# Layer norm, gated MLP and long convolution with gradients: tile 0's norm reordered, tiles 4 and 5 turned by transfers

## The chip, the cores and the metric

One core of a Trainium2 chip. The time is device microseconds of one execution, the median of three timed runs. A separate, profiled execution gives the trace; its times count from the start of its span.

The names are those of the profile. PE is the matrix engine, PEld its weight loads, DVE the vector engine, ACT the scalar engine, POOL the general-purpose engine, and SP the engine that here does nothing but issue transfers. SP's transfers run on queue q1, ACT's on q10, POOL's on q0; all share 16 DMA engines. A transfer is issued by an instruction in the issuing engine's own order, and lands later.

## The reference

The forward pass normalizes the rows of an input, feeds them to a long convolution (branch A) and to a gated MLP (branch B), and adds the results to the input. The kernel returns this output and the gradients of nine inputs for a given `grad_out`.

```
x  = A_q                                  # 2048 x 1024
xn = (x - mean(x)) / sqrt(var(x) + 1e-5)  # per row
A  = xn * (causal_conv(kv, ssm_k) + kv * ssm_D),   kv = shift_conv(k, shift_k) * v
gate, up = xn @ W_gate, xn @ W_up         # 1024 x 3584 each
B  = (relu(gate) * up) @ W_down           # 3584 x 1024
out = x + A + B
grads = vjp of the above for grad_out
```

## The kernel before

The 2048 rows are 16 row tiles of 128. All is bf16 with fp32 accumulation in PSUM. PE runs almost without a pause in this order: `hidden` (gate, up and the gradient of the hidden layer), `grad_down`, `grad_in`, `out_phase`, `grad_x`. Matmuls of branch A are put between those of the first three, at a pace counted in estimated nanoseconds.

The part that is changed is the first of the 14 passes of `hidden` (n = 0, rows 0 to 1023, first 512 of the 3584 hidden columns). For each of its eight row tiles s it needs:

- `gate(s)` and `up(s)`: eight 128x512 matmuls each, with the transposed normalized tile `xnT` as weights and `wg` or `wu` as moving operand (`gemm8`, the matmul at line 1092). ACT takes relu of the gate result, DVE masks the up result and multiplies.
- `grad_row(s)`: eight matmuls with the transposed gradient tile `goT` as weights and `wdT` as moving operand. ACT copies the result to `gh`, DVE multiplies it into the stored pair `ru`.

In this pass nothing is there beforehand: the input tiles are loaded (`ln_load`), normalized (`layer_norm`), transposed (`flip_xn`) and used. `layer_norm` is a generator, and each `next(ln)` moves it one step on; `chunk` takes several steps. Tiles 0 to 3 are normalized singly, the others in pairs. For tile 0, DVE makes mean and variance (`stats`); `root` adds epsilon on DVE and takes the root, and a scaled copy, on ACT; `inverse` makes the reciprocal on DVE. `sums` is an ACT pass with an accumulated sum, and tile 1's mean and variance come from three such passes.

`flip_xn(st)` has two ways. Tiles 0 to 5: eight PE transposes into PSUM (line 1135), then copies to `xnT` by DVE, or by ACT for tile 4 (line 1140). Tiles 6 and 7: a transposing transfer from the normalized tile to `xnT`, issued by SP (line 1128). `goT` and `wdT` are always made by transposing transfers from DRAM.

The order on PE before is: 12 warming matmuls, tile 0's transposes, gate 0, half of up 0, then (by `first_mid`, called after the fourth matmul of up 0) tile 1's transposes, gate 1, up 1, tile 2's transposes, the other half of up 0, gate 2, half of up 2, tile 3's transposes, the other half, gate 3, up 3. Gradient rows 0 and 1 follow, with the transposes of tiles 4 and 5 in the middle of row 1 (`flip_ahead(0)`), then gates and ups 4 and 5, gradient rows 2, 3, 4 and 5 (with `flip_ahead(2)`, which issues the transfers of tiles 6 and 7), gates and ups 6 and 7, and gradient rows 6 and 7.

The order of the work on each engine comes from a scheduler with priorities (`Pri`); instructions given to `keep_in_program_order` stay as written, and `issue_after` puts a bound on when a transfer may be issued. Each engine runs its queue in order. SP's queue at the start is: half of input tile 0, `wg` x4, `wu` x2, input tile 2, `wu` x2, tile 3, `wdT` x2, tiles 4 and 5 in one transfer, `wdT` x2, `goT` 0 and 1, tiles 6 and 7 in one transfer, `goT` 2 and 3, the shift weights `sk_b`, the next pass's `wg` x4, `goT` 4 to 7, `xnT` 6 and 7, the next `wu` x4.

Branch A starts its own loads at a pace set in `ABranch.steps`: filter, gradient (`load_g`), v (`load_v`, tile `vt`), k (`load_taps`), normalized rows (`load_xn`, tile `xt`, read back from DRAM).

Of the kernel before, what the change touches and what calls it, by code (L numbers as in the profile page):

```python
# [14 lines left out]
ALU = mybir.AluOpType  # L15
ACT = mybir.ActivationFunctionType
AX = mybir.AxisListType
P = 128
# [3 lines left out]
class Pri:  # L22
# [9 lines left out]
    def pin(self, ins, always=False):  # L32

        if self.strict or always:
            self.tc.keep_in_program_order(ins)
# [13 lines left out]
class ABranch:  # L49
# [545 lines left out]
    def steps(self):  # L595

        sk_t = self.shift_rows()
        self.pin = True  # L600
        yield 10000
        self.load(self.sk_d, sk_t[:])
        yield 25000
        self.sts = [dict(gi=gi, cg=slice(gi * P, (gi + 1) * P)) for gi in range(self.NG)]
        st = self.sts[0]
        self.load_filter(st)
        self.issue()
        yield 3400
        self.load_g(st)
        yield 3400  # L610
        self.load_v(st)
        yield 3400
        self.load_taps(st)
        yield 6800
        self.load_xn(st)
        self.pin = False
        self.pri.strict = True
        self.open_arena()
        for st in self.sts:
            for p, d in self.slots(st, st["gi"]):  # L620
                *more, last = self.parts(p)
                for fs in more:
                    self.tensor(fs)
                    yield self.DENSE[0]
                self.tensor(last)
                self.run(d)
                self.stores()
                for e in self.queue:
                    e[2] -= 1
                if self.queue and self.queue[0][2] <= 0 and not self.hold():  # L630
                    self.issue()
                yield self.DENSE[p is None] if self.dense else self.SLOT
        while self.out:
            self.stores()
# [238 lines left out]
class LnMlp:  # L873
# [7 lines left out]
    def open_left(self):  # L881
        tc = self.tc
        self.per = tc.alloc_tile_pool(name="b_per", bufs=1, side="left")
        self.actp = tc.alloc_tile_pool(name="b_act", bufs=1, side="left")
        self.w2 = tc.alloc_tile_pool(name="b_w2", bufs=1, side="left")
        self.e2 = tc.alloc_tile_pool(name="b_e2", bufs=6, side="left")
        self.e1 = tc.alloc_tile_pool(name="b_e1", bufs=6, side="left")
        self.ps = tc.alloc_tile_pool(name="b_ps", bufs=8, space=bass.MemoryType.PSUM)
        self.ln_x, self.xn, self.todo, self.kept, self.hold, self.busy = [], [], [[]], [], False, False
        self.rstd = self.per.tile([P, self.ST], F32, name="rstd")  # L890
        self.ident = self.per.tile([P, P], BF16, name="ident")
        make_identity(self.nc, self.ident[:])
# [55 lines left out]
    def layer_norm(self, xn_d, jpool, jtag, spool):  # L948
# [9 lines left out]
        def sums(out, x, func, **kw):  # L958
            jk = jpool.tile([P, D], BF16, name="ln_j", tag=jtag)
            return act(jk[:, 0:x.shape[-1]], x, func, accum_out=out, **kw)  # L960
# [12 lines left out]
            else:  # L973
                quarter(V.tensor_scalar(out=sm[:, 5, 0:n], in0=smb[:, 2, 0:n], scalar1=0.25, scalar2=None, op0=ALU.mult))

        def inverse(sm, smb, n, st0, pin):
            pin(V.reciprocal(out=sm[:, 6, 0:n], in_=sm[:, 4, 0:n]))
            if n == 1:
                V.scalar_tensor_tensor(out=smb[:, 3, 0:n], in0=sm[:, 6, 0:n], scalar=sm[:, 5, 0:n], in1=sm[:, 4, 0:n],
                                       op0=ALU.mult, op1=ALU.add)  # L980
            else:
                V.tensor_tensor(out=sm[:, 5, 0:n], in0=sm[:, 5, 0:n], in1=sm[:, 6, 0:n], op=ALU.mult)
                V.tensor_tensor(out=smb[:, 3, 0:n], in0=sm[:, 4, 0:n], in1=sm[:, 5, 0:n], op=ALU.add)
            self.ln_dve = V.reciprocal(out=self.rstd[:, st0:st0 + n], in_=smb[:, 3, 0:n])
# [24 lines left out]

        for _ in stats(x0, b0):  # L1010
            pass
        sums(s1[:, 0, 0:1], x1[:, 0:h], ACT.Copy, scale=-1.0 / D)
        root(s0, b0, 1, hold, None)
        hold(V.tensor_scalar(out=b0[:, 3, 1:2], in0=b0[:, 0, 0:1], scalar1=-1.0, scalar2=None, op0=ALU.mult))
        hold(V.tensor_scalar(out=x0[:, 0:h], in0=x0[:, 0:h], scalar1=b0[:, 0, 0:1], scalar2=None, op0=ALU.subtract))
        hold(act(x0[:, h:D], x0[:, h:D], ACT.Identity, bias=b0[:, 3, 1:2]))
        hold(sums(s1[:, 1, 0:1], x1[:, h:D], ACT.Copy, scale=-1.0 / D))
        hold(act(b1[:, 0, 0:1], s1[:, 1, 0:1], ACT.Identity, bias=s1[:, 0, 0:1]))
        hold(sums(s1[:, 2, 0:1], x1, ACT.Square, bias=b1[:, 0, 0:1]))
        inverse(s0, b0, 1, 0, hold)  # L1020
        self.pri.now()
        for k in range(2):
            hold(scale(x0[:, k * h:k * h + h], 0))
# [11 lines left out]
        st0 = 2  # L1035
# [88 lines left out]

    def flip_xn(self, st):
        xT = self.act_tile("xnT", st)
        if st > 5:
            self.turned = self.nc.sync.dma_start_transpose(out=xT[:].rearrange("p (a b) -> p a b", b=P),
                                                           in_=self.xn[st])
            return xT  # L1130
        h = self.DT // 2 if st < 3 else self.DT
        for k0 in range(0, self.DT, h):
            pst = self.ps.tile([P, self.DT, P], BF16, name="pst_x", tag="bps")
            for kt in range(k0, k0 + h):
                self.pri.pin(self.nc.tensor.transpose(pst[:, kt, :], self.xn[st][:, kt * P:(kt + 1) * P],  # L1135
                                                      self.ident[:]), always=True)
            c = h // 2 if st == 0 and k0 == 0 else h
            for k in range(k0, k0 + h, c):
                copy = self.nc.scalar.copy if st == 4 else self.nc.vector.tensor_copy
                self.copied = copy(out=xT[:, k * P:(k + c) * P], in_=pst[:, k:k + c, :].rearrange("p a b -> p (a b)"))  # L1140
                if st < 5:
                    self.tc.keep_in_program_order(self.copied)
        return xT

    def warm(self, n):
# [9 lines left out]
    def hidden(self, first, goT, load, ln, tables, Wg, Wu, Wd, g, xn_d, h_d, ug_d):  # L1155
# [6 lines left out]
        for n in range(N):  # L1162
# [69 lines left out]
            def first_rows():  # L1232

                held = []

                def first_mid():
                    flip(2)
                    for _ in range(3):
                        next(ln)
                    gate(1, True)  # L1240
                    next(ln)
                    up(1, after={7: third_tile}, put=lambda f, g: (f(), held.append(g)), hold=True)

                def third_tile():
                    flip(3)
                    next(ln)
                    next(ln)

                def last_mid():
                    flip(4)  # L1250
                    for f in held[0:2]:
                        f()
                    chunk(1)
                    held[2]()
                    chunk(1)
                gate(0)
                yield from step()
                up(0, None, {3: first_mid}, lambda *fs: held.extend(fs), True)
                for _ in range(3):
                    yield from step()  # L1260
                gate(2)
                chunk(1)
                yield from step()
                up(2, last_mid)
                chunk(1)
                yield from step()
                gate(3, True)
                yield from step()
                up(3, hold=True)
                yield from step()  # L1270
# [107 lines left out]
            for sp in range(0, HS, 2):  # L1378
                self.pri.now()
                while len(gT) < min(sp + 4, HS):  # L1380
                    gT.append(self.load_T(g, len(gT), "goT", HS + len(gT)))
                if ahead or sp < HS - 4:
                    if not ahead:
                        load_down(sp // 2)
                        yield from gate_up(sp)
                        if sp:
                            self.hold = False
                        elif fb:
                            self.busy = False
                    if not ahead or sp != 4:  # L1390
                        yield from grad(sp)
                    if ahead and sp == 2:
                        yield from grad(4)
                elif sp == HS - 4:
                    yield from last_rows(sp)
                if ahead:
                    with self.tc.issue_after(self.stored.ins):
                        if sp == 0:
                            load_gate()
                if ahead and sp in (2, 6):  # L1400
                    with self.tc.issue_after(self.put.ins):
# [374 lines left out]
def kernel(  # L1776
# [54 lines left out]
    first.append(b.col_block(B_W_up, 0, "wu", 1, lambda: load(2)))  # L1831
    load(3)
    first.append(b.row_block_T(B_W_down, 0, "wdT", 2, lambda: load(4)))
    goT = [b.load_T(g, i, "goT", 8 + i) for i in range(2)]
    load(5)
    goT += [b.load_T(g, i, "goT", 8 + i) for i in range(2, 4)]
    a.load_shift()
    ln = b.layer_norm(xn_d, a.tmp, "tmp", a.sm)
    def mlp():
# [52 lines left out]
```

## Time and profile before

| | |
|---|---|
| median of the timed runs | 1856.39 us (1855.12 to 1856.97) |
| the profiled execution, in all | 1853.44 us |
| its span | 1851.7 us |
| PE busy | 1845.4 us |
| DVE / ACT / POOL busy | 1114.9 / 644.1 / 34.9 us |
| granted PE clock | 1.00 |
| PE's waits: for the warming operand, for tile 0, for tile 1's copy | 1.5, 1.3, 0.3 us |
| 16 transposes of tiles 4 and 5 | 26.66 to 27.55 us |
| gate row 4 / gate row 6 start | 28.41 / 42.23 us |

A row of a timeline reads: start, length (us), engine, line, operation, output<-input, tile shapes, how often in a row, and in brackets the idle time of the engine just before it and what ended it. Successive matmuls overlap: a 128x512 one is listed with 379 ns, but they start 216 ns apart. On the rows of SP the length is that of the issue, not of the transfer. A row of waits reads: who waited for whom, us in total, times, longest. A row of a DMA queue reads: packets, MB, share of the 16 engines' time.

### The profile page before, as it was taken

Reading aid. Unit: us, or ns where it says so; the run is one execution under the profiler, and the core shown is the slowest. Engines: PE = TensorE matmul, PEld = TensorE weight load, DVE = VectorE, ACT = ScalarE, POOL = GpSimd, SP = SyncE. Lnnn points to the kernel's source line nnn. Section 1 sums busy time; section 2 is a strip of 40 time slices with the busy share of each in tenths; the row PEclk is TensorE's granted clock in tenths of the full one; section 3 lists DMA queues with packets and bytes.
Section 4 is the critical chain, followed back from the end, with each engine's and each line's share of the span. In section 5 each row is a group of like instructions: output and inputs, shape, how many; then the busy total and the mean of one; then the engine's idle time right before and its main releaser. Section 6 shows DMA issues by size and latency. Waiting matters only on the chain.

```text
span 1851.7 us, 32071 instructions
## 1 busy us (share of the span) xinstructions
PE 1845.4 (100%) x13045; PEld 845.8 (46%) x13045; DVE 1114.9 (60%) x1632; ACT 644.1 (35%) x1213; POOL 34.9 (2%) x73
## 2 busy tenths in 40 slices
PE   9999999999999999999999999999999999999999
PEld 4444444444444444444444444444444544444444
DVE  6646797698789768585785667721212222566652
ACT  5644444445444454544544455320000000111100
POOL 2200000000000000000000000000000000000000
PEclk9999999999999999999999999999999999999999
DMA  9997679878767856549566544379999757799863
GB/s 250 276 215 192 152 173 230 208 177 203 174 170 199 243 144 177 143 120 256 152 171 146 149 121 147 119 227 249 261 230 261 179 145 168 174 215 212 207 149 74
DMA packets 746660, 345.17 MB, mean 186 GB/s; under 512 B 577944, under 2 KB 715152, under 8 KB 746512
## 3 DMA queue, kind: packets, MB, share of 16 engines
q1 hardware_dynamic: 732848, 311.39, 70.7%
q10 hardware_dynamic: 9504, 17.04, 2.9%
q0 software_dynamic: 4160, 14.68, 2.3%
q8 instruction: 102, 1.67, 0.4%
q14 instruction: 46, 0.38, 0.1%
HBM read 143.79 MB, written 103.83 MB: 134 GB/s over the span
## 4 chain that ended last, share of the span: by engine, by line
PE 99%; DMA 0%; DVE 0%; issue 0%; ACTq 0%; ACT 0%; DVEq 0%
PE ps_x L1742 21%; PE ps_w L1445 20%; PE ps_g L1092 11%; PE ps_u L1092 11%; PE ps_h L1092 11%; PE ps_o L1610 10%; PE ps_d L1445 9%; PE ps_c L83 4%; PE ps_d L1461 2%; PE ps_w L1461 1%; PE ps_r L1644 0%; DMA ln_x<-in_A_q_dram 0%; PE pst_x L1135 0%; DVE xnT L1140 0%; DVE rest L1648 0%
## 5 line engine op out<-in xcount | busy, mean ns | idle before, releaser
L1445 PE MATMUL ps_w<-ugs,xn_nat 128*128 128x512 bf16 x1728 | 381.1, 379 | 0.0
L87 ACT CAST arena<-ps_c 128x512 bf16<-128x512 f32 x576 | 293.9, 612 | 85.5 <-PE ps_c L83 85.0
L1092 PEld LDWEIGHTS <-xnT 128*128 128x128 bf16 x1792 | 171.7, 98 | 209.0 <-issue 5.2
L1445 PEld LDWEIGHTS <-xn_nat 128*128 128x128 bf16 x1728 | 165.3, 98 | 201.1 <-issue 6.7
L341 DVE STREAM_TRANSPOSE arena<-arena 128x1024 f32<-128x1024 f32 x96 | 180.3, 1934 | 126.3 <-ACT arena L87 108.4
L1092 PE MATMUL ps_u<-wu,xnT 128*128 128x512 bf16 x896 | 205.8, 379 | 0.0
L1092 PE MATMUL ps_g<-wg,xnT 128*128 128x512 bf16 x896 | 205.1, 379 | 0.4 <-DVE xnT L1140 0.3
L1092 PE MATMUL ps_h<-wdT,goT 128*128 128x512 bf16 x896 | 203.6, 379 | 0.0
L1742 PE MATMUL ps_x<-wgT,ggT 128*128 128x512 bf16 x896 | 198.6, 379 | 0.0
L1742 PE MATMUL ps_x<-wuT,guT 128*128 128x512 bf16 x896 | 198.6, 379 | 0.0
L1760 ACT ACTIVATE w<-xn,m 128x512 f32<-128x512 bf16 x32 | 24.3, 807 | 482.5 <-DVE m L1753 369.1
L1610 PE MATMUL ps_o<-wd,hT 128*128 128x512 bf16 (+1 forms) x896 | 187.6, 372 | 0.0
L1445 PE MATMUL ps_d<-g_nat,hs 128*128 128x512 bf16 x768 | 169.9, 379 | 0.0
L1742 PEld LDWEIGHTS <-guT 128*128 128x128 bf16 x896 | 87.7, 98 | 105.7
L1742 PEld LDWEIGHTS <-ggT 128*128 128x128 bf16 x896 | 87.7, 98 | 105.5
L1092 PEld LDWEIGHTS <-goT 128*128 128x128 bf16 x896 | 86.5, 98 | 104.2 <-issue 1.2
L1340 ACT CAST gh<-ps_h 128x512 bf16<-128x512 f32 x112 | 66.2, 591 | 193.6 <-PE ps_h L1092 183.0
L1610 PEld LDWEIGHTS <-hT 128*128 128x128 bf16 x896 | 87.7, 98 | 99.9
L1448 ACT CAST wi<-ps_w 128x512 bf16<-128x512 f32 x108 | 64.6, 598 | 189.9 <-PE ps_w L1445 152.7
L1212 DVE SCALAR_TENSOR_TENSOR ru<-ru,ps_u 128x512 bf16<-128x512 bf16 x112 | 76.5, 683 | 80.7 <-PE ps_u L1092 40.4
L1602 DVE TENSOR_TENSOR ya<-ya,xe 128x1024 bf16<-128x1024 bf16 x16 | 11.1, 692 | 178.2 <-DMA xe<-xn_d 178.2
L91 DVE TENSOR_TENSOR t<-arena 128x2048 bf16<-128x2048 bf16 x96 | 113.9, 1220 | 0.4
(145 smaller groups left out, 1405.5 us busy)
## 6 DMA issues: line engine op xcount, KB each, us to landing
ugs<-ug_d SPq DMA_DIRECT2D x112, 256.0 KB
ug_d<-ru SPq DMA_DIRECT2D x104, 256.0 KB
wg<-in_B_W_gate_dram SPq DMA_DIRECT2D x56, 256.0 KB
wu<-in_B_W_up_dram SPq DMA_DIRECT2D x56, 256.0 KB
hs<-h_d SPq DMA_DIRECT2D x56, 256.0 KB
out_dram<-wi SPq DMA_DIRECT2D x56, 256.0 KB
h_d<-ht SPq DMA_DIRECT2D x104, 128.0 KB
gt<-in_grad_out_dram SPq DMA_DIRECT2D x32, 256.0 KB
```

The costliest lines, as they stand in the source:

```text
L83: self.pri.pin(self.nc.tensor.matmul(out, lhsT=lhsT, rhs=rhs, start=start, stop=stop))
L87: self.pri.pin(self.nc.scalar.copy(out=out, in_=in_))
L91: self.pri.pin(self.nc.vector.tensor_tensor(out=out, in0=in0, in1=in1, op=op))
L341: self.pri.pin(self.nc.vector.transpose(out=df[:, c0:c0 + 32, :], in_=sf[:, c0:c0 + 32, :]))
L1092: self.pri.pin(self.nc.tensor.matmul(ps[:], lhsT=xT[:, kt * P:(kt + 1) * P], rhs=w(kt), start=(kt == 0), stop=(kt == self.DT - 1)), always ...
L1212: return self.pri.pin(nc.vector.scalar_tensor_tensor(out=ru[s][:, 1, :], in0=ru[s][:, 0, :], scalar=0.0, in1=ps[:], op0=ALU.is_gt, op1=ALU ...
L1340: self.pri.pin(nc.scalar.copy(out=gh[:], in_=ps[:]))
L1445: self.pri.pin(self.nc.tensor.matmul(ps[:], lhsT=lhsT(st), rhs=rhs(st), start=(st == 0), stop=(st == self.ST - 1)))
L1448: self.pri.pin(self.nc.scalar.copy(out=out, in_=ps[:]))
L1461: self.pri.pin(self.nc.tensor.matmul(ps[i][:], lhsT=lhsT(i, st), rhs=rhs(i, st), start=(st == 0), stop=(st == self.ST - 1)))
L1610: nc.tensor.matmul(ps, lhsT=hT[:, kt, :], rhs=self.wd[:, kt, oc], start=(kt == 0), stop=(kt == self.FT - 1))
L1742: nc.tensor.matmul(ps, lhsT=T[:, kt, :], rhs=W[:, kt, oc], start=(i == 0), stop=(i == n - 1))
```

## The change

Four edits.

1. Tile 0's norm (`layer_norm`). The root and its scaled copy come ahead of tile 1's first sum on ACT. The second half of tile 0 is centred by DVE (`less(h)`, called by `inverse` right after its reciprocal) and no longer by ACT; the DVE instruction that made the negated mean for ACT goes away.
2. The split of up row 0. Tile 1's transposes stay behind its fourth matmul, but gate row 1 and what follows comes behind its sixth; so two matmuls stand between the transposes and gate row 1, and two are left for after tile 2's transposes.
3. Tiles 4 and 5 are turned as tiles 6 and 7 are. The 16 PE transposes, one ACT copy and one DVE copy of 128x1024 go; SP issues two more transposing transfers. In the first pass gradient rows 2 and 3 come directly behind rows 0 and 1, ahead of gate row 4. On SP, `goT` 0 to 3 are issued in a row ahead of the load of tiles 6 and 7; `xnT` 4 and 5 come behind `sk_b`; then `goT` 4 and 5, the next `wg` x4, `goT` 6 and 7, `xnT` 6 and 7. `goT` 4 and later and `wg` are bound to come after the second of the turned tiles.
4. Branch A's first loads: `load_xn` and `load_v` change places; on SP the two `xt` transfers come where the two `vt` transfers were, and the other way round.

PE's queue has 16 matmuls fewer, ACT's two instructions fewer, DVE's one fewer (one copy and one small instruction go, one half-tile subtraction comes), and SP's two more. POOL issues gradient stores 2 and 3 ahead of the hidden stores of rows 4 and 5.

```
@@ steps
-        self.load_v(st)
+        self.load_xn(st)
         yield 3400
         self.load_taps(st)
         yield 6800
-        self.load_xn(st)
+        self.load_v(st)
@@ layer_norm
-        def inverse(sm, smb, n, st0, pin):
+        def inverse(sm, smb, n, st0, pin, amid=None):
             pin(V.reciprocal(out=sm[:, 6, 0:n], in_=sm[:, 4, 0:n]))
+            if amid is not None:
+                amid()
...
-        sums(s1[:, 0, 0:1], x1[:, 0:h], ACT.Copy, scale=-1.0 / D)
+        def less(c):
+            hold(V.tensor_scalar(out=x0[:, c:c + h], in0=x0[:, c:c + h], scalar1=b0[:, 0, 0:1], scalar2=None,
+                                 op0=ALU.subtract))
+
         root(s0, b0, 1, hold, None)
-        hold(V.tensor_scalar(out=b0[:, 3, 1:2], in0=b0[:, 0, 0:1], scalar1=-1.0, scalar2=None, op0=ALU.mult))
-        hold(V.tensor_scalar(out=x0[:, 0:h], in0=x0[:, 0:h], scalar1=b0[:, 0, 0:1], scalar2=None, op0=ALU.subtract))
-        hold(act(x0[:, h:D], x0[:, h:D], ACT.Identity, bias=b0[:, 3, 1:2]))
+        hold(sums(s1[:, 0, 0:1], x1[:, 0:h], ACT.Copy, scale=-1.0 / D))
+        less(0)
         hold(sums(s1[:, 1, 0:1], x1[:, h:D], ACT.Copy, scale=-1.0 / D))
...
-        inverse(s0, b0, 1, 0, hold)
+        inverse(s0, b0, 1, 0, hold, lambda: less(h))
@@ flip_xn
-        if st > 5:
-            self.turned = self.nc.sync.dma_start_transpose(out=xT[:].rearrange("p (a b) -> p a b", b=P),
-                                                           in_=self.xn[st])
+        if st > 3:
+            self.turned.append(self.nc.sync.dma_start_transpose(out=xT[:].rearrange("p (a b) -> p a b", b=P),
+                                                                in_=self.xn[st]))
             return xT
@@ hidden
                 def first_mid():
-                    flip(2)
...
-                up(0, None, {3: first_mid}, lambda *fs: held.extend(fs), True)
+                up(0, None, {3: lambda: flip(2), 5: first_mid}, lambda *fs: held.extend(fs), True)
...
-                    gT.append(self.load_T(g, len(gT), "goT", HS + len(gT)))
+                    with self.tc.issue_after(self.turned[1].ins):
+                        gT.append(self.load_T(g, len(gT), "goT", HS + len(gT)))
...
-                    if not ahead or sp != 4:
-                        yield from grad(sp)
-                    if ahead and sp == 2:
-                        yield from grad(4)
+                    for at in ((0, 2), (4,), (), (6,))[sp // 2] if ahead else (sp,):
+                        yield from grad(at)
...
-                    with self.tc.issue_after(self.stored.ins):
-                        if sp == 0:
+                    with self.tc.issue_after(self.turned[1].ins):
+                        if sp == 2:
                             load_gate()
@@ kernel
-    goT = [b.load_T(g, i, "goT", 8 + i) for i in range(2)]
+    goT = [b.load_T(g, i, "goT", 8 + i) for i in range(4)]
     load(5)
-    goT += [b.load_T(g, i, "goT", 8 + i) for i in range(2, 4)]
```

## The prediction

> **What bounds the kernel now.** First the page's busy times, then PE's waits.
>
> ```profile
> PE 1845.4 (100%) x13045; PEld 845.8 (46%) x13045; DVE 1114.9 (60%) x1632; ACT 644.1 (35%) x1213; POOL 34.9 (2%) x73
> ```
> ```profile
> PE ps_warm L1151 <- POOL warm L1148: 1.5, 1, 1.5
> PE pst_x L1135 <- DVE ln_x L987: 1.3, 1, 1.3
> PE ps_g L1092 <- DVE xnT L1140: 0.3, 1, 0.3
> ```
>
> PE is idle for 6.3 us of 1851.7: 3.1 us in these three waits, all before 12 us, and nearly all of the rest after its last matmul, which ends at 1848.7. So only two things can help: fewer PE instructions, or less waiting in the first 12 us. Any new wait of PE goes straight to the end, as nothing later has slack to give back. Everything that the change touches for PE lies before 53 us, so I read that stretch in time order; ACT and DVE first, with the transposes that they hold up:
>
> ```profile
> 5.21 0.63 ACT L955 ACTIVATE ln_j<-ln_x 128x512 bf16<-128x512 bf16 x1 [2.04 <-DMA ln_x<-in_A_q_dram]
> 5.83 0.28 ACT L955 ACTIVATE ln_s<-ln_b 128x1 f32<-128x1 bf16 x2
> 6.05 0.16 DVE L977 RECIPROCAL ln_s<-ln_s 128x1 f32<-128x1 f32 x1 [0.49 <-ACT ln_s L955]
> 7.20 0.66 PE L1135 MATMUL pst_x<-ident,ln_x 128*128 128x128 bf16 x8 [1.32 <-DVE ln_x L987]
> ```
>
> Tile 0's root (the ACT pair at 5.83) waits behind a sum of tile 1 that came first. Then PE around tiles 4 and 5, and the sync queue SP, whose issues follow each other with hardly a gap from 17.3 to 39.2 us:
>
> ```profile
> 24.07 2.75 PE L1092 MATMUL ps_h<-wdT,goT 128*128 128x512 bf16 x12
> 26.66 1.06 PE L1135 MATMUL pst_x<-ident,ln_x 128*128 128x128 bf16 x16
> 27.55 1.03 PE L1092 MATMUL ps_h<-wdT,goT 128*128 128x512 bf16 x4
> ```
> ```profile
> 17.30 2.67 SPq L1116 DMA_TRANSPOSE goT<-in_grad_out_dram  x2
> 20.15 1.47 SPq L943 DMA_DIRECT2D ln_x<-in_A_q_dram  x1
> 21.67 3.85 SPq L1116 DMA_TRANSPOSE goT<-in_grad_out_dram  x2
> 25.57 0.60 SPq L237 DMA_DIRECT2D sk_b<-in_A_shift_k_dram  x1
> 26.21 2.12 SPq L1085 DMA_DIRECT2D wg<-in_B_W_gate_dram  x4
> 28.37 7.61 SPq L1116 DMA_TRANSPOSE goT<-in_grad_out_dram  x4
> 36.09 3.08 SPq L1128 DMA_TRANSPOSE xnT<-ln_x  x2
> ```
>
> The last row is normalized tiles 6 and 7, turned by transfers already. The DMA view of the single microsecond from 41 shows when their data ends, and PE's timeline who needs tile 6:
>
> ```profile
> q1 hardware_dynamic: 126, 0.02, 12.4%
> ```
> ```profile
> 42.23 3.62 PE L1092 MATMUL ps_g<-wg,xnT 128*128 128x512 bf16 x16
> ```
>
> SP's queue (q1) moved 1933 packets from 38 to 41 us, some 640 per us; the 126 after 41 end at about 41.2. The second issue ended at 36.09 + 3.08 = 39.2, so data ends 2.0 us behind its issue. Tile 6 (the second issue starts at 37.5) is there at about 39.5, and gate row 6 asks for it at 42.23: 2.7 us of slack.
>
> **Tile 0's norm.** Root and copy now precede tile 1's sum on ACT, and ACT's centring of the second half goes to DVE, between reciprocal and the fused step behind it. The root can start when DVE's add ends, 5.08 + 0.16, so at about 5.28 instead of 5.83. DVE: first half 5.16 to 5.51 (0.35 as now), reciprocal to 5.67, second half 0.35 more, partly in the 0.28 us that now pass between reciprocal and fused step; that step starts at about 5.9 instead of 6.33. PE's first transposes: 0.45 us earlier, 6.75. Tile 1's chain on ACT loses the 0.70 us centring ahead of its second sum, so its tile is ready about 0.5 us earlier too (PE now waits for it until 10.79). ACT is left with less, DVE with 0.35 - 0.15 us more, inside the same waits.
>
> **Up row 0 split at 6.** Two of its matmuls (216 ns apart) move between tile 1's transposes and gate row 1, where PE now waits 0.3 us for the DVE copy; they would cover it. Their weights are wu's third piece: q1's bytes, added up in half microseconds, reach it at 9.6 us, and they are asked for at 10.7. The tail behind tile 2's transposes shrinks from 0.86 to 0.43 us, against a copy whose first half is there about 0.9 us after the first transpose (10.79 to 11.70 for tile 1) and 0.45 us of transposes: 0.03 us may show. Following tiles 2 and 3, whose norms then bind (both end within 0.2 us of PE's asking now), I get gate row 2 0.9 us and gate row 3 0.8 us earlier. I take -0.8 for both edits together; -0.3 if the norms of tiles 2 and 3 bind fully, -1.0 if nothing does.
>
> **Tiles 4 and 5.** 16 PE transposes go. They hold PE from 26.66 to 27.55: 0.89 us, 56 ns each. The two copies of 1.01 us (ACT) and 0.68 us (DVE) go too; PE doesn't wait for them, so nothing. Gradient rows 2 and 3 (16 matmuls, 3.45 us) change places with gate row 4 and what follows; no PE work is added. So far -0.8 - 0.89 = -1.7, and PE would ask for tile 4 at 24.07 - 0.8 + 4 x 1.73 = 30.2, for tile 5 at 31.9, for tile 6 at 42.23 - 1.7 = 40.5.
>
> What is added is on SP: two transposes of tiles 4 and 5 before gradient rows 4 to 7 and the next wg. SP's order becomes goT 0 to 3, tiles 6 and 7's load, sk_b, tiles 4 and 5, goT 4 and 5, wg x4, goT 6 and 7, tiles 6 and 7. goT 2 is asked for at 26.7 and its issue would be over by 21.3. The load of tiles 6 and 7 comes behind two more transposes, some 2.7 us later; their norm's first ACT sum (28.21 now) then waits for it, and gradient evictions 1 to 3 wait behind that on ACT by about 2 us, which eight PSUM banks cover. Tile 4 itself is ready at DVE's last scale, 25.43 + 0.44 now, 25.1 then; SP reaches it at 17.30 + 4 x 1.34 + 1.47 + 0.60 and the gaps, 24.9, so its issue ends near 26.6 and its data near 28.6 to 29.4. Tile 5 comes 1.5 us later: 0.8 to 1.6 us in time.
>
> The wait goes on to tile 6. Ahead of its transpose SP has two more of about 1.49 us (median of the two xnT<-ln_x issues): 37.5 + 2.97 + 2.0 = 42.4, against 40.5 asked for. PE waits 1.9 us at gate row 6. Tile 7 follows 1.5 us later, less than gate row 6's 1.73, so it adds nothing; behind tile 6 on PE stand gates and ups 6 and 7 and gradient rows 6 and 7, and all of the rest. Once PE waits there, the sum is simply the arrival less 42.23, whatever the first 30 us gained. Bounds: goT streams from 17 to 21 us at 289 GB/s, 0.91 us for 262144 bytes, and the empty microsecond from 21 to 22 might be filled, which gives 37.5 + 1.8 - 1.0 + 2.0 = 40.3, no wait; the longest xnT issue of the trace is 2.75 us, which gives 45.0. I take the median, as the same kind of transfer from the same place.
>
> [...]
>
> **xt ahead of vt.** Two pairs of loads change places near 118 us; PE waits for neither side. Nothing, bounded by the 4.0 us between the two (118.28 and 122.27) either way if PE had no lead there; it shows no wait after 12 us, so I keep none of it.
>
> **Sum.** -1.7 + 1.9 = +0.2 us on the profiled span of 1851.7. That execution took 1853.44 us in all; the median of the three timed runs is 1856.39, so I add the difference to the median: 1856.6.
>
> **Rivals.** A is the above.
> B: the turned tiles land in time. For it: the empty microsecond, and 0.91 us a tile. Against: SP's average of 1.72 us a transpose in this stretch (17.2 us for ten). -1.7: 1854.7.
> C, slower: SP and its transfers fall behind at tiles 4 and 5 already. Each of the two extra transposes takes 2.75 us, tile 6 comes at 45.0, and PE is idle for 4.5 us. For it: DMA engines are over 100% busy in most of this stretch, and goT's longest issue is 3.39. Against: both SBUF-sourced ones took under 1.71. A PE that has stood idle starts slowly, as at the start of this trace, where eight warming weight loads come 0.43 us apart before the distance halves: 8 x 0.21 = 1.7 us more. 45.0 - 42.23 + 1.7 = +4.5: 1860.9. [...]
> [...]
>
> ```profile
> 3.57 0.15 PEld L1151 LDWEIGHTS <-warm 128*128 128x128 bf16 x1 [0.28 <-issue]
> 4.00 0.15 PEld L1151 LDWEIGHTS <-warm 128*128 128x128 bf16 x1 [0.28 <-issue]
> 4.85 0.53 PEld L1151 LDWEIGHTS <-warm 128*128 128x128 bf16 x3 [0.28 <-issue]
> ```
>
> D: the start doesn't get faster (the norms of tiles 1 to 3 set it) and tile 6 is in time: -0.89: 1855.5.
> E: a transpose costs its whole 219 ns (1.06 us is 16 of them overlapped). Then 16 x 0.219 = 3.5 go, and with -0.8 it is 1852.1 when tile 6 is in time. Against: the next matmul starts 0.89 us after the first transpose. [...]
>
> **How the numbers follow.** A 54%, B 23%, C 15%, D 5%, E 3%. 0.2% is 3.7 us, about what a measurement of this kernel can tell from no change. A's own range: 0.9 to 2.0 us for each extra transpose, 1855.5 to 1857.7. The range goes down to B less 0.6 for scatter of a median (the runs lie 1.9 apart), 1854.1, and up to C's arrival without the cold clock, 42.23 to 45.0, 1859.2. Faster: E and a sliver of B, 4%. Slower: C nearly whole, 12%. Same 84%.
>
> **What would show it.** First transposes at 6.75 and gate row 3 at 19.8 (start); no transposes between gradient rows; a PE wait for a DMA at gate row 6 of 1 to 3 us, with gate row 6 starting at 42.4; no wait at gate rows 4 and 5. Wrong if PE waits at gate row 4, if the last q1 data of tile 7 ends before 42, or if PE waits anywhere after 53 us.

## The result and the profile after

| | before | after |
|---|---|---|
| median of the timed runs | 1855.76 us (1854.60 to 1857.96) | 1862.06 us (1861.46 to 1864.15) |
| profiled execution, in all | 1853.44 us | 1861.86 us |
| its span | 1851.7 us | 1860.0 us |
| gate row 6 of the first pass starts | 42.23 us | 45.71 us |
| gate row 0 of the second pass starts | 52.59 us | 60.58 us |

The changed kernel is slower: 1.0036 times the time before, 95% interval 1.0026 to 1.0046, or 6.3 us. The two profiled executions differ by 8.3 us in span, because that of before lies 2.3 us below its own median.

PE's start times say where the 8 us arise. The second pass begins 7.99 us later; `grad_down` begins at 637.25 instead of 629.28, `out_phase` at 1276.16 instead of 1268.20, `grad_x` at 1463.58 instead of 1455.61. The distance stays at 8.0 us, so all of it comes before 61 us, and edit 4 near 118 us has no part in it. The view of PE's waits, of after:

```profile
PE ps_g L1098 <- DMA xnT<-ln_x: 5.4, 3, 4.1
PE ps_warm L1156 <- POOL warm L1153: 1.5, 1, 1.5
PE pst_x L1141 <- DVE ln_x L991: 0.3, 1, 0.3
```

The wait for tile 0's norm has gone from 1.3 to 0.3 us, and a wait that was not there leads the list: gate rows wait three times for turned tiles. PE's timeline of after shows which:

```profile
6.84 0.66 PE L1141 MATMUL pst_x<-ident,ln_x 128*128 128x128 bf16 x8 [0.31 <-DVE ln_x L991]
...
30.27 1.89 PE L1098 MATMUL ps_g<-wg,xnT 128*128 128x512 bf16 x8
32.79 1.90 PE L1098 MATMUL ps_g<-wg,xnT 128*128 128x512 bf16 x8 [0.63 <-DMA xnT<-ln_x]
...
37.98 3.62 PE L1098 MATMUL ps_h<-wdT,goT 128*128 128x512 bf16 x16
45.71 3.59 PE L1098 MATMUL ps_g<-wg,xnT 128*128 128x512 bf16 x8 [4.11 <-DMA xnT<-ln_x]
50.01 3.59 PE L1098 MATMUL ps_g<-wg,xnT 128*128 128x512 bf16 x8 [0.71 <-DMA xnT<-ln_x]
53.39 3.89 PE L1098 MATMUL ps_u<-wu,xnT 128*128 128x512 bf16 x16
```

The start does what edits 1 and 2 say (first transposes at 6.84, not 7.20), and gate row 4 is where the moved gradient rows put it. Then tile 5 is 0.63 us late, tile 6 4.11 us, tile 7 0.71 us. Gate rows 6 and 7 last 3.59 us instead of 1.90: every matmul takes twice as long. The reason stands in the granted clock (the third column from the end) of a view by half microseconds, of after:

```profile
43.00:43.50 0.50, 0.00 (x0) 0.00 (x0) 0.00 (x1) 0.00 (x0) 0.20 (x1) 1.00 0.96 214
43.50:44.00 0.50, 0.00 (x0) 0.00 (x0) 0.00 (x0) 0.00 (x0) 0.50 (x2) 0.70 1.24 273
...
53.50:54.00 0.50, 0.50 (x3) 0.20 (x2) 0.00 (x0) 0.36 (x1) 0.00 (x0) 0.56 0.46 70
54.00:54.50 0.50, 0.50 (x4) 0.20 (x2) 0.00 (x0) 0.23 (x1) 0.00 (x0) 1.00 0.83 233
```

PE is idle from 41.60 (37.98 + 3.62). A mean clock of 0.70 in the half microsecond from 43.5 puts the fall to 0.50 at 43.7; by the same working it is back at 53.94.

The 8.0 us add up along PE's path. Gate row 7 starts when tile 7 is there, 50.01 instead of 42.23 + 1.73 = 43.96: +6.05. It then takes 3.38 us (to 53.39) instead of 1.73: +1.65. Up rows 6 and 7 take 3.73 us instead of 3.45: +0.28. The slow gate row 6 (3.59 us instead of 1.90) is no term of its own, since PE would have waited for tile 7 in that time anyway. So most of the loss is two late tiles, and 1.9 us of it the clock.

SP's queue shows how the tiles became late (timeline of after; the length is that of the issues):

```profile
25.25 3.49 SPq L1134 DMA_TRANSPOSE xnT<-ln_x  x2
28.79 3.65 SPq L1122 DMA_TRANSPOSE goT<-in_grad_out_dram  x2
32.49 2.21 SPq L1091 DMA_DIRECT2D wg<-in_B_W_gate_dram  x4
34.74 6.44 SPq L1122 DMA_TRANSPOSE goT<-in_grad_out_dram  x2
41.28 3.39 SPq L1134 DMA_TRANSPOSE xnT<-ln_x  x2
```

SP reaches tile 4 at 23.45 and stands idle until 25.25, when the tile is normalized. Tiles 4 and 5 are issued in 3.49 us, the two `goT` behind `wg` take 6.44 us, and tiles 6 and 7 are issued 5.2 us later than before (41.28, not 36.09). Tile 6's issue ends at 42.5 and PE starts on it at 45.71; tile 7's ends at 44.7 and PE starts at 50.01. Before, data ended 2.0 us behind the issue. The queues' share of the 16 DMA engines in the microsecond from 44, of after:

```profile
q0 software_dynamic: 92, 0.32, 87.0%
q1 hardware_dynamic: 133, 0.03, 16.3%
```

POOL's stores (q0) have 3.5 KB per packet, SP's transposes (q1) 0.2 KB, and the engines spend their time on the stores. Such stores ran beside tiles 6 and 7 in the kernel before too, but fewer. POOL's queue in the five microseconds from the start of their issues, before (36 to 41 us) and after (41 to 46 us):

```profile
q0 software_dynamic: 96, 0.26, 17.7%
```
```profile
q0 software_dynamic: 247, 0.78, 45.1%
```

### The profile page after: what moved, and what is told of

It is laid out like the page before. It is cut to its first block, busy times and chain, and to the rows that moved or that the text cites. A ratio compares the mean times of both kernels' runs of the same rounds, so it can differ in the third digit from the quotient of the medians.

```text
span 1860.0 us, 32036 instructions
## 1 busy us (share of the span) xinstructions
PE 1849.3 (99%) x13029; PEld 845.6 (45%) x13029; DVE 1114.2 (60%) x1631; ACT 642.8 (35%) x1211; POOL 34.9 (2%) x73
## 4 chain that ended last, share of the span: by engine, by line
PE 98%; DMA 1%; DVE 0%; ACT 0%; issue 0%; SPq 0%; ACTq 0%
PE ps_x L1745 21%; PE ps_w L1448 20%; PE ps_g L1098 10%; PE ps_u L1098 10%; PE ps_h L1098 10%; PE ps_o L1613 10%; PE ps_d L1448 9%; PE ps_c L83 4%; PE ps_d L1464 2%; PE ps_w L1464 1%; DMA xnT<-ln_x 1%; PE ps_r L1647 0%; DMA ln_x<-in_A_q_dram 0%; ACT ln_j L955 0%; PE pst_x L1141 0%
```

## The experiments

Start with the parts alone. Base and edit are named with each; a ratio is to the kernel before on the same chip.

**Edits 1 and 2 alone**, put into the kernel before.

```
-        inverse(s0, b0, 1, 0, hold)
+        inverse(s0, b0, 1, 0, hold, lambda: less(h))
...
-                up(0, None, {3: first_mid}, lambda *fs: held.extend(fs), True)
+                up(0, None, {3: lambda: flip(2), 5: first_mid}, lambda *fs: held.extend(fs), True)
```

> The kernel before with edits 1 and 2 alone (tile 0's norm, the split of up row 0). Theory: the start gives what the changed trace shows, gate row 3 at 19.9 instead of 20.6, and nothing takes it back, as tiles 6 and 7 had 2.7 us in hand: 0.7 us faster than before, 1855.1. Rival: the sync queue does not move with PE and the gain is eaten at tile 4 or 6: no change.

1854.23 us (1852.65 to 1855.88), ratio 0.9999 (0.9991 to 1.0008). Gate row 3 starts at 19.96 instead of 20.60, and PE is still 0.64 us ahead at 107 us; no gate row waits. The gain is in the trace, and in the time it can't be told from no change.

**Edit 4 alone**, put into the kernel before.

```
-        self.load_v(st)
+        self.load_xn(st)
...
-        self.load_xn(st)
+        self.load_v(st)
```

> The kernel before with edit 4 alone (xt ahead of vt). Theory: PE waits for neither, no new wait in PE's list and no change, 1853.5 to 1856.5. Rival: a wait of PE near 110 to 140 us, and a time over 1857.

1853.64 us (1853.43 to 1857.91), ratio 0.9997 (0.9988 to 1.0007), no new wait. It is worth nothing that can be measured.

**Edits 3 and 4 without 1 and 2.**

```
-        inverse(s0, b0, 1, 0, hold, lambda: less(h))
+        inverse(s0, b0, 1, 0, hold)
...
-                up(0, None, {3: lambda: flip(2), 5: first_mid}, lambda *fs: held.extend(fs), True)
+                up(0, None, {3: first_mid}, lambda *fs: held.extend(fs), True)
```

> The changed kernel without edits 1 and 2 (start as before). Theory (the end is set by when tile 6 arrives): tile 4 is normalized 0.7 us later, SP waited for it (idle from 23.45 to 25.25), so all of SP's later issues move by 0.7 at most; tile 6 arrives at 45.7 to 46.4, and the time is 1862 to 1863, while PE alone would put it 0.7 later in any case. Rival (the shortened start caused the loss by bringing PE ahead of its transfers): gate row 6 is not waited for, and the time is below 1858.

1860.88 us (1857.23 to 1864.13), ratio 1.0035 (1.0021 to 1.0048): the loss is edit 3's. The profiled execution is the fastest of the four. There gate row 4 waits 0.75 us and gate row 6 2.61 us, tile 6 is used at 45.05, 0.6 us earlier than forecast, and the clock stays at 1.00. The other three lie at 1860.07 to 1864.13; their mean granted clocks are 0.999, 0.997 and 0.998 (after: 0.997 and 0.998), so in them the clock fell for a while.

**Tiles 4 and 5 by PE again, everything else as after**, `wg` still in the middle of the `goT`. The bound that let `goT` 4 and later and `wg` start only behind the second turned tile goes too.

```
-        if st > 3:
+        if st > 5:
...
+                    if ahead and len(gT) == 6:
+                        load_gate()
```

> The changed kernel with tiles 4 and 5 turned by PE as before; SP's order is that of the changed kernel without these two transposes, wg between gradient transfers 5 and 6. Theory (the two transposes ahead of tile 6 are what is too much): tile 6 arrives 3 to 4 us earlier than 45.7, at about 42, against gate row 6's 41.5; a wait of 0 to 1 us, and a time within 1 us of before. Rival (the place of wg is the fault): a wait of 3 us or more stays, with a time over 1857.

1853.89 us (1852.70 to 1854.25), ratio 0.9998 (0.9988 to 1.0007). PE's timeline:

```profile
38.07 3.62 PE L1098 MATMUL ps_h<-wdT,goT 128*128 128x512 bf16 x15
41.52 3.62 PE L1098 MATMUL ps_g<-wg,xnT 128*128 128x512 bf16 x16
```

Gate rows 6 and 7 follow gradient row 5 without a wait. With `wg` in its new place but without the two added transposes nothing is late: the transposes, with the bound that hangs on them, are needed for the loss, and `wg`'s place alone does no harm. SP's idle time ahead of tile 4, which is gone here as well, does not decide: in the trace of `puts_late` below it is 0.1 us, and tile 6 is used at 48.68.

**The clock: 22 useless matmuls ahead of gate row 6**, which keep PE at work while tile 6 is on its way.

```
+                    if end:
+                        ps = self.ps_tile("ps_warm")
+                        for _ in range(22):
+                            self.pri.pin(nc.tensor.matmul(ps[:], lhsT=xT[5][:, 0:P], rhs=wu(0), start=True, stop=True),
+                                         always=True)
```

> The changed kernel with 22 matmuls of no use (into a PSUM tile that nobody reads) ahead of gate row 6, so that PE is busy for 4.75 us of its wait. Theory (part of the loss is the clock, which is 0.50 from 46 to 53 us because PE stood idle for over 4 us): gate row 6 starts at 46.2, takes 1.73 us instead of 3.59, PE then waits for tile 7 until it arrives at 50.0, and all else runs at full speed; 1.9 us faster than the changed kernel, 1860.2. Rival (slow matmuls there have another cause, such as transfers that take SBUF's time): gate rows 6 and 7 still take 3.4 to 3.6 us each, and the kernel is no faster than 1862.

1860.67 us (1859.60 to 1863.69), ratio 1.0036 (1.0023 to 1.0049). That is the ratio of after, so the time shows nothing of the 1.9 us expected; the trace does. PE's timeline:

```profile
46.88 1.90 PE L1098 MATMUL ps_g<-wg,xnT 128*128 128x512 bf16 x8 [1.00 <-DMA xnT<-ln_x]
50.99 1.90 PE L1098 MATMUL ps_g<-wg,xnT 128*128 128x512 bf16 x8 [2.21 <-DMA xnT<-ln_x]
```

The clock stays at 1.00 and both gate rows take 1.90 us: the idle PE had caused their 3.59 us. But tile 6 comes 1.2 us later than in after, and gate row 7 now waits 2.21 us for tile 7. The second pass starts at 59.63: of the 8.0 us of after, 7.0 remain at full clock. The clock is the smaller part of the loss; the arrival of tiles 6 and 7 is the larger one.

**What makes tile 6 late: `wg` behind the turned tiles.** Its four loads, 1 MB, move from the place after `goT` 5 to behind tile 7.

```
+                    if end:
+                        with self.tc.issue_after(self.turned[3].ins):
+                            load_gate()
...
-                if ahead:
-                    with self.tc.issue_after(self.turned[1].ins):
-                        if sp == 2:
-                            load_gate()
```

> The changed kernel with one edit: the four wg loads for the next pass are issued behind the turned tiles 6 and 7 and no longer between gradient transfers 5 and 6. My theory (SP's queue q1 is served in order; 1 MB of wg and the start of a transpose behind plain loads made tile 6 arrive at 45.7): tiles 6 and 7 then arrive before 40 and 42 us, PE waits at most 0.6 us (at gate row 5), the clock stays at 1.00, gate row 6 starts near 41.4 and the kernel is 1.2 us faster than before, 1854.5. Rival (the two extra transposes alone are too much, wherever wg is): a wait of 1 to 3 us stays at gate row 6, 1856 to 1859. Second rival (wg becomes late instead): no wait at gate row 6, but one for wg at the first gate row of the next pass, near 51 us.

1854.96 us (1853.58 to 1857.77), ratio 1.0004 (0.9995 to 1.0013). PE's timeline:

```profile
32.66 3.63 PE L1098 MATMUL ps_g<-wg,xnT 128*128 128x512 bf16 x16 [2.28 <-DMA xnT<-ln_x]
...
43.03 3.62 PE L1098 MATMUL ps_g<-wg,xnT 128*128 128x512 bf16 x16
```

Gate row 6, which asks 1.4 us later than in after, waits no more, and the clock stays at 1.00. But the issues of tiles 4 and 5 took 5.26 us here, and gate row 4 waits 2.28 us, which eats the gain.

**Two pieces of `wg` ahead, two behind** tile 7.

```
-                            load_gate()
+                            load_gate(0)
...
+                            load_gate(1)
```

> The changed kernel with two of the four wg loads behind turned tile 7 and two left between gradient transfers 5 and 6. [...] Rival (what counts is that a plain load stands there at all, for the change from plain to transposing): as with four, a wait of 4 us, 1860 to 1862.

1855.81 us (1854.29 to 1859.14), ratio 1.0004 (0.9995 to 1.0013). Gate row 6 starts at 43.26 after a wait of 1.43 us, clock 1.00. With four pieces ahead, gate row 6 starts at 45.05, 45.71, 46.88 and 48.68 in four traces (`turn_only`, after, `warm_wait`, `puts_late`); with two at 43.26; with none it doesn't wait. Tile 6 is later the more of `wg` comes before it; as four traces alike in this differ by 3.6 us, what one piece costs is not shown.

**`wg` directly behind tile 5**, ahead of `goT` 4 to 7.

```
-                        if sp == 2:
+                        if sp == 0:
```

> The changed kernel with the four wg loads directly behind turned tile 5, ahead of gradient transfers 4 to 7 (as they stood ahead of these in the kernel before); the same transfers are ahead of tile 6, in another order. Theory (what counts is how much q1 has to move before tile 6): tile 6 arrives at 44.5 to 46.5 as in the changed kernel, PE waits 3 to 5 us at gate row 6, and the time is 1858 to 1863. Rival (wg in the middle of the transposes is the fault, by the two changes between plain and transposing): tile 6 arrives by 43, and the time is below 1857.

1857.16 us (1856.34 to 1859.05), ratio 1.0018 (1.0008 to 1.0028). Neither case came as written: gate row 6 starts at 44.96, but it waits for nothing. The wait moved to gradient row 4:

```profile
39.66 5.31 PE L1098 MATMUL ps_h<-wdT,goT 128*128 128x512 bf16 x16 [2.31 <-DMA goT<-in_grad_out_dram]
```

Whatever stands behind `wg` and the two transposes is the late one. These 16 matmuls take 5.31 us, not 3.62: the clock fell to 0.50 at 40.58, 0.9 us behind an idle time of PE of 2.31 us (last section).

**POOL's part: thin stores.** In the first pass the stores of rows 0 to 5 move 8 of 128 partitions; behind row 7 the rest is written, from row 7's tile.

```
-                    self.put = queue.dma_start(out=ug_d[r:r + P, :, cols], in_=t[:])
+                    e = 8 if n == 0 and r < 6 * P else P
+                    self.put = queue.dma_start(out=ug_d[r:r + e, :, cols], in_=t[0:e])
+                    if n == 0 and r == 7 * P:
+                        for i in range(6):
+                            queue.dma_start(out=ug_d[i * P + 8:i * P + P, :, cols], in_=t[8:P])
```

(`h_d` in the same way.)

> The changed kernel with POOL's stores of rows 0 to 5 of the first pass cut to 8 of 128 partitions (the rest of these rows is written behind row 7, with row 7's values, so the output is not the reference's). Their 2.3 MB no longer run beside the transposes of tiles 4 to 7. Theory (POOL's transfers, with larger packets, slow down SP's transposes of 256-byte packets on the shared DMA engines): tile 6 arrives at 43 to 44 instead of 45 to 48.7, and PE waits 1.5 to 3 us at gate row 6, with the clock at 1.00. Rival (the order on SP alone sets the arrival): it still comes after 45 and the clock falls. The time itself says little here, as the late stores run beside the loads of the next pass.

PE's timeline:

```profile
37.08 3.62 PE L1098 MATMUL ps_h<-wdT,goT 128*128 128x512 bf16 x16
42.16 3.63 PE L1098 MATMUL ps_g<-wg,xnT 128*128 128x512 bf16 x15 [1.46 <-DMA xnT<-ln_x]
```

Tile 6 comes 3.55 us earlier than in after and 2.9 us earlier than in the earliest of the four traces above, earlier than the 43 to 44 expected, with `wg` where the change put it; gate row 5 doesn't wait. The issues of `goT` 4 to 7 and `wg` ahead of tile 6 take 9.8 us (28.29 to 38.08), as in the kernel before (9.9), where those four traces have 10.2 to 12.5. So POOL's stores beside the transposes are the third ingredient, on the word of one trace. The time, 1863.23 us (two runs, 1862.99 and 1863.46), says nothing of this: behind the stores put off, PE waits 2.0 us for ACT at 84 us and 3.4 us for `wu` from 102 us on; why is not shown.

**POOL's three stores of `xn_d` put off** behind gradient row 7.

```
-                if ahead and sp in (2, 6):
+                if ahead and sp == 6:
...
-                        for put in self.kept[0:3] if sp == 2 else self.kept[3:7]:
+                        for put in self.kept[0:7]:
```

> The changed kernel with POOL's three stores of normalized tiles 1 to 3 (768 KB, issued from 43.9 us) put behind gradient row 7, with the other four. Theory (tile 7 arrived at 50.0, 5.3 us after its issue ended at 44.7, because the transfers of those stores share the DMA engines): tile 7 arrives 2 us earlier, by 48, gate row 7 does not wait, and the time is 0.7 us below the changed kernel. Gate row 6 still waits over 3 us. Rival (a transpose in this place is slow by itself): gate row 7 still waits until 50.

1860.45 us (1858.65 to 1863.18), ratio 1.0027 (1.0015 to 1.0040). In its trace gate row 4 waits 1.63 us, and tile 6 comes later still: gate row 6 starts at 48.68 after a wait of 6.25 us, though these stores are issued at 43.9 in after, when tile 6 was already on its way. Gate row 7 doesn't wait, but gate row 6 runs at half clock and covers 3 us. Queue q1 moves nothing from 49.5 us on, so here tile 7 lies at most 0.8 us behind tile 6, and not 4.3 us as in after. That speaks for the theory, but with tile 6 so late one trace doesn't settle it.

**Looking for a version that is faster than both.** From `wg_last`, the kernel with `wg` behind, three edits: the load of `sk_b` moved behind `wg` too; tile 4 by PE and only tile 5 by a transfer; both by PE (run twice).

```
+                            self.branch.load_shift()
...
-    a.load_shift()
```
```
-        if st > 3:
+        if st > 4:
```
```
-        if st > 3:
+        if st > 5:
```

> The kernel with wg last, and the small load of the shift weights (8 KB in 1024 packets of 8 bytes) moved behind wg too, so that nothing stands between the load of tiles 6 and 7 and turned tile 4. There gate row 4 waited 2.3 us for tile 4. Theory (those packets take about a microsecond of the queue ahead of tile 4): the wait at gate row 4 falls to about 1.2 us and the time by as much, 1853.5. Rival (gradient transfers 0 to 3 and the load are what is ahead of it): the wait stays near 2 us, 1854.5.

1855.51 us (1854.20 to 1860.13), ratio 1.0009 (1.0000 to 1.0018). The wait at gate row 4 is gone (it starts at 30.24), and in its place gradient rows of the second pass wait 0.55 and 3.35 us for `wdT`, in an execution of 1858.55 us.

> The kernel with wg last, but tile 4 turned by PE as before and only tile 5 by a transfer. Tile 5 is then first behind the load of tiles 6 and 7 and arrives when tile 4 did there, 30.3 to 32.7; gate row 5 asks for it at 23.3 + 0.45 + 5 x 1.73 = 32.4. Theory (a turned tile is worth it only where its arrival is hidden): a wait of 0 to 0.3 us for 0.45 us of transposes saved, so within 0.4 us of the kernel with both by PE, 1853.0 to 1853.5. Rival (it arrives later, as contention moves it from run to run): a wait over 0.5 us, and 1854 or more.

1853.99 us (1852.34 to 1858.42), ratio 1.0002 (0.9993 to 1.0011). No gate row waits for a turned tile; PE is 1.4 us ahead of before at 61 us and 0.7 us at `grad_down`.

> Edits 1, 2 and the new order (gradient rows 2, 3 ahead of gate row 4, wg last), but tiles 4 and 5 turned by PE as before. Theory (the order costs nothing, the transfers of tiles 4 and 5 cost a wait of 2.3 us for the 0.9 us of transposes that they save): no wait of PE after 12 us, 0.6 us faster than before, 1853.9, and 1 us faster than the kernel with wg last. Rival (the order itself brings waits, as gradient tiles 2 and 3 are asked for 7 us earlier): PE waits at gradient row 2 or 3, and the time is not below that of the kernel with wg last.

1853.16 us (1852.67 to 1858.59), ratio 0.9995 (0.9986 to 1.0004).

> The kernel with edits 1, 2, the new order, wg last and tiles 4 and 5 by PE, once more, for its interval. Theory: 0.6 us of the start is kept, as PE has no wait after 12 us: 0.6 us (0.03%) faster than before, and the interval of the ratio may still hold 1. Rival: no gain at all, the median within 0.2 us of before.

1855.51 us (1853.01 to 1859.58), ratio 1.0008 (1.0000 to 1.0017), the same kernel as the one above. Its trace has a wait of 0.9 us for `wu`, which the first one hasn't; the 0.6 us expected don't show in the time. So none of these three kernels is shown to be faster than before; by their ratios they stand 0.3 to 0.4% below the change (1.0036).

## Why the prediction was wrong, step by step

- **What bounds the kernel, "any new wait of PE goes straight to the end"**: right. The 8.0 us at 61 us are still 8.0 us at 1463 us.
- **Tile 0's norm, up row 0**: right. First transposes at 6.84 (6.75 forecast), gate row 3 at 19.91 (19.8).
- **16 PE transposes and the moved gradient rows**: right. Gate row 4 asked for tile 4 at 30.27 (30.2 forecast). From the first matmul of gradient row 0 to gate row 4 PE takes 7.80 us with both tiles turned by PE (`pe45_wg_mid`, 23.36 to 31.16), 7.35 with one (`tile5`, 23.15 to 30.50), 6.90 with none (after, 23.37 to 30.27): 0.45 us a tile, 56 ns a transpose. The rival of 219 ns each is out.
- **"0.8 to 1.6 us in time" for tiles 4 and 5**: half wrong. The start of their issue was well forecast (25.25 against 25.1 for the last scale), and tile 4 was in time. Tile 5 was forecast for 30.1 to 30.9 and used at 32.79, 0.63 us late and 4.05 us behind the end of its issue (28.74), not 2.0.
- **The wait at gate row 6**: this step failed. The place was right, and so was the kind of cause, two more transposes ahead of tile 6; but its sum, 37.5 + 2.97 + 2.0 = 42.4, was too small by 3.3 us. The issues of the added transposes took 2.08 and 1.31 us, near 1.49. What was priced as unchanged was not. `goT` 4 to 7 and `wg` between them and tile 6 took SP 12.5 us (28.79 to 41.28) and not 9.9 (26.21 to 36.09), so tile 6's issue ended at 42.5, where the sum has 40.5. And its lag behind that was 3.2 us, not 2.0. So it came at 45.7. Pushed back, these transfers met more of POOL's stores, 0.78 MB in five microseconds for 0.26. `wg_last`, `thin_stores` and `pe45_wg_mid` each take away one of three (`wg` ahead, stores, transposes), and tile 6 comes in time, at 42.2, and in time.
- **"goT streams from 17 to 21 us at 289 GB/s, 0.91 us"**, the lower bound and a reason for case B: misread. In the trace of before that rate holds until 18.6 (287 GB/s in the microsecond from 17 us); the mean from 17 to 21 us is 220 GB/s, 1.19 us for as many bytes.
- **"Tile 7 follows 1.5 us later ... so it adds nothing"**: wrong too. It came 4.3 us later; `warm_wait` shows the wait of 2.21 us that a gate row 6 at full clock would leave.
- **Case C** comes near in the time, 1860.9 us (1862.06), and partly by luck. Its arrival of 45.0 (45.7) rested on 2.75 us for each added issue (2.08 and 1.31), not on what they do to those behind them. Its 1.7 us for the slow PE (1.9 on the path) were meant for gate row 6, whose slowness cost nothing; gate row 7 and the ups paid. It has nothing for tile 7, which put 2.6 us on top of tile 6 (6.05 less 45.71 - 42.23). In all it has 4.5 us, where the two traces differ by 8.0. In after the clock fell 2.1 us into the wait of 4.11 us. The range ended ahead of its clock term.
- **Edit 4 at nothing**: right, as `xt_only` shows.

## What to carry to other kernels

Price a transfer that is added to a full queue by the arrival of the last thing behind it, with the loads and stores that it is pushed into, not by the duration of its own issue. Where 0.89 us of PE work is handed to such a queue, look for the first operand that PE then waits for, and for the one behind that. And a wait of PE may cost a second time through the clock: one of 2.31 us did here, while one of 2.61 us did not.

## What the runs showed of the hardware that was not expected

**In four traces the clock was down for 3.41 us or two or three times that.** From views by half microseconds, each edge worked out as above:

| kernel | PE idle | clock falls | clock is back | down for |
|---|---|---|---|---|
| after | 41.60 to 45.71, and 0.71 us later | 43.70 | 53.94 | 10.24 us |
| puts_late | 42.42 to 48.68 | 47.27 | 54.10 | 6.83 us |
| sk_wg_last | 60.34 to 63.69 | 63.01 | 66.42 | 3.41 us |
| wg_first | 37.35 to 39.66 | 40.58 | 43.99 | 3.41 us |

These are one, two and three times 3.41 us, and the fall comes 2.1 to 4.9 us behind the start of the idle time, in `wg_first` when PE had been at work again for 0.9 us. The same view of `wg_first`:

```profile
40.00:40.50 0.50, 0.50 (x4) 0.20 (x2) 0.00 (x0) 0.00 (x0) 0.00 (x0) 1.00 1.06 427
40.50:41.00 0.50, 0.50 (x3) 0.19 (x2) 0.00 (x0) 0.00 (x0) 0.00 (x0) 0.58 0.92 363
```

PE is busy in all of both half microseconds (second column), and the clock falls in the second. Idle times of 2.61 us (`turn_only`), 2.28 us (`wg_last`) and 2.21 us (`warm_wait`) left it at 1.00. So the length of a wait doesn't decide alone. What else does is not shown.

**POOL's stores hold back SP's transposes** on the shared DMA engines. Between 44 and 45 us of after the stores had 87.0% of the engines' time and SP's transposes 16.3%. In `thin_stores`, six rows of stores (0.39 MB each, by 128 rows x 512 columns x 2 bytes three times) cut to a sixteenth brought tile 6 forward by 3.55 us against after, and by 2.9 us against the earliest of the four traces with whole stores. The stores' packets are larger, 3.5 KB against 0.2 KB; that the size of the packets matters, and not the bytes alone, is not shown.
